# Turning the keys by a transposing transfer and ScalarE in place of TensorE, from the seventh block on

## The chip, the cores and the metric

The kernel runs on one core of one Trainium2 chip. The metric is the time of one execution in device microseconds (us), the median of several runs. Engines are called as in the profile: PE is TensorE (matmuls and transposes), PEld its weight loads, DVE is VectorE, ACT is ScalarE, POOL is GpSimd, and SP is SyncE, which issues the DMA transfers. The engines run side by side; each takes its own instructions in the order fixed when the program is built, and waits on semaphores where it needs another's result.

## What is computed

First a gated linear attention over 4 batches, 8 heads, 768 steps, head size 48, and then a gated MLP with a product along the sequence:

```python
for t in range(S):
    state = alpha[:, :, t, :, None] * state + np.einsum('bhd,bhe->bhde', k[:, :, t], v[:, :, t])
    y[:, :, t] = np.einsum('bhd,bhde->bhe', q[:, :, t], state)
x = y as (batch, 768, 384)
h = gelu_tanh(x @ w_in)                    # 384 -> 1024
u, v = the two halves of h                 # 512 columns each
v_n = (v - mean) / sqrt(var + 1e-06) * g_ln
v_s = np.einsum('ts,bsd->btd', w_sg, v_n) + b_sg
out = x + (u * v_s) @ w_out                # 512 -> 384
```

## The kernel before

**The attention in blocks.** A batch is cut into 6 blocks of 128 steps, 24 blocks in all, numbered i = 0 to 23. The channels of 8 heads lie on 128 partitions, in 3 groups of columns (NK = 3) of 128 steps each; a fourth place per block is filled by two small DMA moves (`last_pair`). For a block the steps are:

- `load_a`, `load_kqv`: the decays and the keys, queries and values come in by DMA.
- `decay` (L405) and `invert` (L427): DVE scans the running product of the decays and its inverse. The inverse lies in a tile with the tag `pi`, of which there are two buffers; that of block i + 2 can be scanned when `scale_k` of block i is done.
- `scale_q` (L418) and `scale_k` (L434): queries times the product, keys times the inverse, in place, 128 x 384 elements each. `scale_k` is the step called ("k", i).
- unit S: 32 small products of keys and queries (L462), masked by DVE (L571).
- unit T: `transposes(i)` turns the scaled keys on PE, three transposes of 128x128 (L566) into PSUM; `k_rows(i)` copies them to the tile `kn` with two ACT copies, of 384 and of 96 elements a partition (L581, L582). This is the step ("kn", i); `kn` has three buffers.
- unit A: products of the masked scores and the values (L477), and the block's gain, values by turned keys (L500, reads `kn`). A waits for the mask and for `kn`.
- units M and H: the rest of the block's output, from the carried state (L477, L488). Between A and M stands `turn` (L544), a tiny ACT instruction that M waits for. DVE then updates the state.

S, A, M and H use 48 or 64 rows of the array and are called tiled here; T and the wide products below use 128.

**The MLP.** Three of the blocks give half a batch's x, split into high and low parts, so that each product is three matmuls (`mm3`, L667 to L669). The wide units are V (x into the second half of h, one per block, followed by GELU, moments, normalisation and a split on ACT, DVE and POOL), U (x into the first half), P (the product along the sequence, 18 matmuls, which needs all six V of the batch) and R (the output product).

**What sets the order.** `ORDER` is a hand-written list of all units of PE. A planner in the kernel (`Plan.issue`) walks through all steps when the program is built: it has a cost in ns for each step, a rule for DMA landings (the issue, plus bytes at 375 a ns, plus 2700 ns for large transfers) and due times from the list; on each engine it takes the step that can start first by its own reckoning, and PE's units at most five places ahead of the list. Several steps have a second engine to go to (`other`), among them the normalisations (ACT or DVE). What comes out is a fixed order of instructions on each engine; at run time only semaphores decide when each starts.

Of the kernel before, what the change touches and what calls it, by code (L numbers as in the profile page):

```python
# [9 lines left out]
F32 = mybir.dt.float32  # L10
F32R = mybir.dt.float32r
BF16 = mybir.dt.bfloat16
I32 = mybir.dt.int32
U32 = mybir.dt.uint32
AF = mybir.ActivationFunctionType
ALU = mybir.AluOpType
PSUM = bass.MemoryType.PSUM

B, H, S, D = 4, 8, 768, 48
DM, DFF = 384, 1024  # L20
HALF = DFF // 2
P = 128
C = 128
C1 = C + 1
NCH = S // C
NP = H // 2
NK = DM // P
# [11 lines left out]
SUMMED = (0, 1)  # L39
EPS = 1e-6  # L40
GEN = 8
LINE, ROOM = 216, 78
NB = 4
SINGLE = 24
R = 64 + D
F64_MIN_AS_F32 = float(np.array(0x38100000, np.uint32).view(np.float32))

ORDER = """
    A0 S0 M0 T2 S2 T0 S1 T1 H0 M1 A1 T3 S3 A2 H2 H1 M2 V01 T4 A3 V00 U002 M3 H3 M4 S4 S5 U000 V02 A4 T5 S6 H4 T7 A5
    T6 A6 S7 V03 H5 M5 M6 V05 U003 A7 H6 V04 M7 P002 P000 S8 H7 U001 U010 P003 U011 U012 T9 P001 U013 P013 T8 P010  # L50
    S9 H8 A9 A8 S10 R000 M8 T10 V10 R002 M9 R001 H9 P011 V12 P012 T11 R011 U101 V13 S11 A10 H10 S12 M10 A11 U103
    R010 M11 A12 V11 H11 M12 H12 T12 S13 U110 U102 T13 V15 P101 V14 U100 U111 R012 P102 A13 P100 S14 P113 P110 R102
    P103 H13 M13 R101 T14 S15 A14 H14 T15 A15 S16 U113 M14 U112 H15 T16 M15 U200 R100 S17 T17 A16 H16 T19 V22 M16
    V24 V20 R112 P111 P112 S18 M17 A17 H17 V21 U201 U202 V23 V25 P200 R110 R111 U203 T18 U210 S19 A19 H18 P203 A18
    S20 M18 T21 H19 P210 T20 M19 R201 P202 P201 R200 U213 A20 S21 T22 U212 A21 H20 S22 M20 H21 U211 P211 U300 M21
    R202 P212 S23 A22 H22 V30 V31 T23 M22 P213 A23 H23 V33 V32 U302 M23 V34 P310 R211 V35 R210 U310 U301 P301 U312
    R212 U311 P313 U313 P312 P302 P300 U303 R302 P303 R311 R300 R301 P311 R310 C0 R312
"""

FIRST = (  # L60
# [131 lines left out]
def tile_gla_gmlp(ctx: ExitStack, tc: tile.TileContext, aT, kqv, w_in, w_sgT, w_out, g_ln, b_sg, out):  # L192
    nc = tc.nc

    const = ctx.enter_context(tc.tile_pool(name="const", bufs=1))
# [6 lines left out]
    att1 = ctx.enter_context(tc.tile_pool(name="att1", bufs=1))  # L202
# [8 lines left out]
    alo2 = const.tile([P, 1], F32, name="alo2")  # L211
    nc.scalar.activation(alo2, warm[:, 0:1], AF.Gelu_apprx_tanh)
    rident = const.tile([P, P], F32R, name="rident")
# [18 lines left out]
    nc.gpsimd.memset(nhalf, -0.5)  # L232
    low = const.tile([P, B * NCH + LINE], F32, name="low")[:, 0:B * NCH]
    pend = const.tile([P, B * NCH, NK], F32, name="pend")
    s_c = const.tile([P, 2, NP, D], F32, name="s_c")
    s_m = const.tile([P, 2, NP, D], F32, name="s_m")

    wi_hi = const.tile([P, 2, NK, HALF], F32R, name="wi_hi")
    wi_lo = const.tile([P, 2, NK, HALF], F32R, name="wi_lo")
# [43 lines left out]
    def split_f64(dst_hi, dst_lo, src, by_pe):  # L283
# [6 lines left out]
        def mag():  # L290
            t["mag"] = stage.tile([P, TH], F32, tag="mag", name="mag", bufs=2)

        def bounded():
            mag()
            nc.scalar.activation(t["mag"], t["raw"][:, :, 1].bitcast(F32), AF.Abs)
            nc.vector.tensor_scalar_max(t["mag"], t["mag"], F64_MIN_AS_F32)
# [20 lines left out]
        def rest():  # L317
            nc.vector.scalar_tensor_tensor(
                dst_lo if by_pe else t["mag"], t["raw"][:, :, 0].bitcast(U32), 2.0 ** -52, t["mag"], op0=ALU.mult, op1=ALU.mult,
            )  # L320
# [58 lines left out]
    st = {}  # L379
    xs = {}  # L380
    groups = [(i,) for i in range(SINGLE)] + [(i, i + 1) for i in range(SINGLE, B * NCH, 2)]

# [38 lines left out]
    def invert_end(i):  # L421
        nc.vector.reciprocal(ends[:, :, C], st[i]["pf"][:, :, C])

    def invert(i):
        s = st[i]
        s["pi"] = pi = att1.tile([P, NK, C1], F32, tag="pi", name="pi", bufs=2)
        nc.vector.tensor_tensor_scan(  # L427
            pi.rearrange("p j t -> p (j t)")[:, ::-1], s["a"][:, NK * C1:0:-1],
            ends.rearrange("p j t -> p (j t)")[:, ::-1], initial=0.0, op0=ALU.mult, op1=ALU.max,
        )  # L430

    def scale_k(i, eng):
        k = st[i]["k"][:, 1:]
        eng.tensor_tensor(k, k, st[i]["pi"][:, :, 1:], op=ALU.mult)  # L434
# [5 lines left out]
    def range_low(i):  # L440
        av = st[i]["a"][:, 0:NK * C1].rearrange("p (j t) -> p j t", t=C1)[:, :, 1:]
        nc.scalar.activation(av, av, AF.Relu, bias=alo, scale=-1.0, accum_out=low[:, i:i + 1])

# [9 lines left out]
    def group(i):  # L453
        return groups[of_group[i]]

    def place(i):
        return group(i).index(i)
# [66 lines left out]
    def carries(i):  # L524
        return i % NCH < NCH - 1
# [33 lines left out]
    def needed(i):  # L559
        return C if carries(i) else 64  # L560
# [16 lines left out]
    def k_rows(i):  # L577
        s = st[i]
        s["kn"] = kn = att1.tile([P, NK * P + 2 * D], F32, tag="kn", name="kn", bufs=3)
        n, tp = needed(i), s["tp"]  # L580
        nc.scalar.copy(kn[0:n, 0:NK * P].rearrange("t (k d) -> t k d", k=NK), tp)  # L581
        nc.scalar.copy(  # L582
            kn[0:n, NK * P:].rearrange("t (e r k) -> t e r k", e=2, k=NK),
            tp.rearrange("t k (e d) -> t e d k", e=2)[:, :, D:],
        )

    def keep_warm(o, n):
        n_col = o.shape[-1]
        moving = warm[:, 0:n_col] if n_col <= P else warm[:, None, :].to_broadcast([P, n_col // P, P])
        for _ in range(n):  # L590
            nc.tensor.matmul(o, warm, moving, start=True, stop=True, skip_group_check=True)

    def state_half(i, on_act=False):
        m = place(i)
        d0, mid = st[group(i)[0]]["dl0"][0:R, m], s_m[0:R, m]
        if i % NCH > 0:
            nc.vector.tensor_tensor(mid, s_c[0:R, m], d0, op=ALU.add)
        elif on_act:
# [4 lines left out]
    def state_add(i):  # L603
        m = place(i)
        nc.vector.tensor_tensor(s_c[0:R, place(i + 1)], s_m[0:R, m], st[group(i)[0]]["dl1"][0:R, m], op=ALU.add)

    def state_decay(i, eng):
        carried = s_c[0:R, place(i + 1)]
        eng.tensor_tensor(carried, carried, st[i]["kq"][0:R, :, 2 * C, None].to_broadcast([R, NP, D]), op=ALU.mult)

# [61 lines left out]
    def mlp_v(x, t, c, summed=False):  # L672
# [7 lines left out]
        def gelu():  # L680
            t["vg"] = mlp.tile([P, HALF], F32, tag="vg", name="vg", bufs=2)
            nc.scalar.activation(t["vg"], t["o"], AF.Gelu_apprx_tanh)

# [17 lines left out]
        def norm_act():  # L701
            nc.scalar.activation(t["vg"], t["vg"], AF.Identity, bias=t["off"], scale=t["rstd"])

# [13 lines left out]
        def gelu_sum():  # L717
            t["vg"] = mlp.tile([P, HALF], F32, tag="vg", name="vg", bufs=2)
            t["sum"] = mlp.tile([P, 2], F32, tag="mv", name="sum", bufs=2)
            nc.scalar.activation(t["vg"], t["o"], AF.Gelu_apprx_tanh, accum_out=t["sum"][:, 0:1])  # L720

# [193 lines left out]
    plan = Plan()  # L915
# [15 lines left out]
    def unit(token):  # L931
# [6 lines left out]
        if kind == "C":  # L938
            return ("R", B - 1, 1, NK - 1, 0), 0
        return (kind, *map(int, rest)), {"U": 1574, "P": 3161, "V": 2091, "R": 2090}[kind]  # L940
# [4 lines left out]
    t = 5000.0  # L945
# [9 lines left out]
    for name, p in pieces:  # L955
        def at(k, name=name):
            return (k,) + name

        if "shift" not in p:
            if name[2] == 1:  # L960
                plan.add(at("load"), "sp", 330, p["load"], takes=[("raw", 2, [at("low")])], nbytes=196608)
            else:
                k = name[1]
# [4 lines left out]
                    takes=[("gl" if k else "gh", 1, [("low", "ws", x, 0) for x in blocks])] if k % ND == 0 else [],  # L968
                    nbytes=196608, due=FIRST.index(("ws", k)) * 20000 - 10**6,
# [14 lines left out]
        last = at("low_pe") if on_pe else at("low")  # L984
# [29 lines left out]
    def first(name):  # L1014
        return FIRST.index(name) * 20000 - 10**6 if name in FIRST else None

    for i in range(n):
# [3 lines left out]
        last = not carries(i)  # L1021
# [3 lines left out]
            nbytes=198656, due=first(("a", i)) or due["S", g[0]] - 15000 + 3000 * m,  # L1025
# [3 lines left out]
            takes=[("kqv", NB, [("H", i)] + ([] if last else [("state", i)]))],  # L1029
            nbytes=394752 if apart else 599552, due=first(("kqv", i)) or due["S", g[0]] - 12000 + 3000 * m,  # L1030
        )
        if apart:
# [5 lines left out]
            takes=[("pf", 2, [("q", i), ("pend", i), ("kept", i), ("end", i)])],  # L1038
# [2 lines left out]
        plan.add(("kept", i), "pool", 100, lambda i=i: decay_kept(i), [("scan", i)])  # L1041
        plan.add(("q", i), "dve*", 550, lambda i=i: scale_q(i), [("scan", i), ("kqv", i)])
        plan.add(("end", i), "dve", 150, lambda i=i: invert_end(i), [("scan", i)] + ([("recip", i - 1)] if i > 0 else []))
        plan.add(("recip", i), "dve*", 960, lambda i=i: invert(i), [("end", i)], takes=[("pi", 2, [("k", i)])])
        by_dve = ("dve*", 550, lambda i=i: scale_k(i, nc.vector))
        by_pool = ("pool", 1150, lambda i=i: scale_k(i, nc.gpsimd))
        plan.add(("k", i), *by_dve, [("recip", i), ("kqv", i)], other=by_pool if b > 0 else None)
# [6 lines left out]
        made = ("A", g[0])  # L1054
        if m == 0:
# [2 lines left out]
            plan.add(  # L1058
                ("turn", i), "act", 190, lambda g=g: turn(g), [made], lead={made: (SLOT if last else 2 * SLOT) - 60 + 410 * len(both[1:])}, keen=300,
            )  # L1060
        plan.add(("kn", i), "act", 740 if not last else 700, lambda i=i: k_rows(i), [("T", i)], takes=[("kn", 3, [made])])
        carried = [("state", i - 1)] if c > 0 else []
        plan.add(
            ("half", i), "dve", 350, lambda i=i: state_half(i), [made] + carried + read_of("m", i), keen=400,
# [2 lines left out]
        if not last:  # L1067
# [13 lines left out]
            takes=[("xf", 3, users)] if head else [],  # L1081
        )
        for e in range(2):
# [3 lines left out]
            takes=[("xh", 2, readers)] if head else [],  # L1087
# [13 lines left out]
    for name, ns in units:  # L1101
        kind, i = name[:2]
# [31 lines left out]
    for b in range(B):  # L1134
# [22 lines left out]
        for hf in range(2):  # L1157
            x = xs[b, hf]
            h = (b, hf)
            for d in range(ND):  # L1160
                u, p = ("U", b, hf, d), ("P", b, hf, d)
# [40 lines left out]
            for kk in range(NK):  # L1202
                r = ("R", b, hf, kk)
# [7 lines left out]
                if (b, hf, kk) == (B - 1, 1, NK - 1):  # L1211
                    for k in range(2):
                        s = st_[4](k)
                        name = r if k == 1 else r + (0,)
# [19 lines left out]
    for k, src in enumerate(words):  # L1234
        t = {}
# [30 lines left out]
    end = due[("P", B - 1, 1, 0)]  # L1266
# [100 lines left out]
```

## Time and profile before

| | |
|---|---|
| time, three runs | median 351.18 us (349.92 to 351.61) |
| span of the profiled execution | 348.3 us; its own time is not listed apart |
| PE busy | 339.9 us, 98% of the span |
| DVE busy | 238.2 us, 68% |
| ACT busy | 156.2 us, 45% |
| POOL busy | 50.0 us, 14% |
| instructions | 10779 |

The span runs from the first to the last instruction of the profiled execution; a run's time has some 2.9 us more around it. A busy time counts an engine's instructions without overlap. In lists of groups a row gives line, engine, operation, tile written <- tiles read, shape, count, then busy us and mean ns of one, and idle time before them with what ended it.

### The profile page before, as it was taken

To read this page: it belongs to the slowest core of one execution; us is meant where nothing else is said; L and a number is where in the kernel's file an instruction comes from. 1 tells how busy PE (TensorE), PEld (TensorE's weight loads), DVE (VectorE), ACT (ScalarE), POOL (GpSimd) and SP (SyncE) were. 2 spreads that over 40 slices of the span, in tenths; PEclk is the share of its full clock that TensorE was granted. 3 is DMA by queue.
4 is the path that set the end of the run, shared out by engine and by line. 5 is a ranking of instruction groups with operands and counts; after the bars stand their busy time and mean duration, and the time that the engine had idled before them with its cause. 6 is when DMAs were issued, how large, how long until landed. Compare 5 with 4: busy or idle time off the path is not lost. (4 is left out here: it accounts for less than half of the span.)

```text
span 348.3 us, 10779 instructions
## 1 busy us (share of the span) xinstructions
PE 339.9 (98%) x4507; PEld 309.5 (89%) x4507; DVE 238.2 (68%) x484; ACT 156.2 (45%) x423; POOL 50.0 (14%) x127
## 2 busy tenths in 40 slices
PE   8898999999999999999999999999999999999996
PEld 4576788899989988999999979999999889999996
DVE  5997988799998668665756788678434667334432
ACT  4564788864433655731225556354132463211100
POOL 2011513410020211300001133101000043000000
PEclk9999999999999999999999999999999999999999
DMA  7948746754336125421234365476200000000012
GB/s 247 388 152 262 219 125 195 223 161 136 104 98 203 36 68 152 118 66 48 71 115 118 103 185 165 135 236 216 68 9 30 8 8 25 23 26 0 2 36 105
DMA packets 23048, 40.80 MB, mean 117 GB/s; under 512 B 3536, under 2 KB 16976, under 8 KB 22992
## 3 DMA queue, kind: packets, MB, share of 16 engines
q1 hardware_dynamic: 22992, 40.05, 37.2%
q8 instruction: 36, 0.59, 0.7%
q14 instruction: 20, 0.16, 0.2%
HBM read 31.77 MB, written 4.72 MB: 105 GB/s over the span
## 5 line engine op out<-in xcount | busy, mean ns | idle before, releaser
L668 PE MATMUL mm_s<-ws_lo,vh 128*128 128x384 f32 x192 | 65.2, 339 | 0.0
L667 PE MATMUL mm_s<-ws_hi,vh 128*128 128x384 f32 x192 | 65.2, 339 | 0.0
L669 PE MATMUL mm_s<-ws_hi,vl 128*128 128x384 f32 x192 | 64.5, 336 | 0.0
L796 DVE SCALAR_TENSOR_TENSOR g<-mm_s,g_col,b_bc 128x384 f32<-128x384 f32 x32 | 19.6, 613 | 26.7 <-PE mm_s L669 26.7
L667 PEld LDWEIGHTS mm_s<-ws_hi,vh 128*128 128x128 f32 x192 | 36.0, 188 | 0.2
L668 PEld LDWEIGHTS mm_s<-ws_lo,vh 128*128 128x128 f32 x192 | 36.1, 188 | 0.0
L669 PEld LDWEIGHTS mm_s<-ws_hi,vl 128*128 128x128 f32 x192 | 36.0, 188 | 0.0
L667 PE MATMUL mm_u<-xh,wi_hi 128*128 128x384 f32 x96 | 33.2, 345 | 0.0
L669 PE MATMUL mm_u<-xh,wi_lo 128*128 128x384 f32 x96 | 32.3, 337 | 0.0
L668 PE MATMUL mm_u<-xl,wi_hi 128*128 128x384 f32 x96 | 32.2, 335 | 0.0
L667 PE MATMUL mm_v<-wi_hi,xh 128*128 128x512 f32 x72 | 29.2, 405 | 0.0
L667 PE MATMUL mm_o<-gh,wo_hi 128*128 128x384 f32 x84 | 28.7, 342 | 0.0
L669 PE MATMUL mm_v<-wi_hi,xl 128*128 128x512 f32 x72 | 28.3, 394 | 0.0
L668 PE MATMUL mm_o<-gl,wo_hi 128*128 128x384 f32 x84 | 28.2, 336 | 0.1
L668 PE MATMUL mm_v<-wi_lo,xh 128*128 128x512 f32 x72 | 28.2, 392 | 0.0
L804 ACT CAST gh<-g 128x384 fp32r<-128x384 f32 x28 | 14.2, 512 | 31.1 <-DVE g L801 24.9
L669 PE MATMUL mm_o<-gh,wo_lo 128*128 128x384 f32 x84 | 28.2, 335 | 0.0
L768 ACT ACTIVATE u<-mm_u 128x384 f32<-128x384 f32 x32 | 15.7, 490 | 27.0 <-PE mm_u L669 27.0
L825 DVE TENSOR_TENSOR r<-mm_o,xf 128x384 f32<-128x384 f32 x23 | 12.5, 551 | 20.8 <-PE mm_o L669 17.2
L405 DVE TENSOR_TENSOR_SCAN pf<-a,floor 128x387 f32<-128x387 f32 x24 | 22.8, 954 | 2.8 <-DMA a<-in_aT 2.7
L477 PEld LDWEIGHTS y<-at,kqv_t 64*64 64x64 f32 x768 | 16.1, 133 | 8.3 <-issue 5.7
L427 DVE TENSOR_TENSOR_SCAN pi<-a,ends 128x387 f32<-128x387 f32 x24 | 23.0, 957 | 0.1
(141 smaller groups left out, 739.9 us busy)
## 6 DMA issues: line engine op xcount, KB each, us to landing
kqv_t<-in_kqv SPq DMA_DIRECT2D x22, 586.0 KB, 4.2
a<-in_aT SPq DMA_DIRECT2D x30, 194.0 KB, 3.0
raw<-in_w_in SPq DMA_DIRECT2D x14, 384.0 KB, 4.6
out_x<-r SPq DMA_DIRECT2D x23, 192.0 KB, 1.9
raw<-in_w_out SPq DMA_DIRECT2D x8, 384.0 KB, 3.3
kqv_t<-kqv_t SPq DMA_DIRECT2D x48, 48.2 KB, 2.2
raw_sg<-in_w_sgT SPq DMA_DIRECT2D x6, 192.0 KB, 5.9
xf<-y SPq DMA_DIRECT2D x48, 24.0 KB, 2.7
```

Source lines behind the costliest of these rows:

```text
L405: nc.vector.tensor_tensor_scan(pf.rearrange("p j t -> p (j t)"), s["a"][:, 0:NK * C1], floor.rearrange("p j t -> p (j t)"), initial=0.0, o ...
L427: nc.vector.tensor_tensor_scan(pi.rearrange("p j t -> p (j t)")[:, ::-1], s["a"][:, NK * C1:0:-1], ends.rearrange("p j t -> p (j t)")[:, : ...
L477: lambda j=j: nc.tensor.matmul(y_of(y, m, j, e)[:, half(h)], v[half(h), D * (2 * j + e):D * (2 * j + e) + 64], at[half(h), e, m, j], start ...
L667: nc.tensor.matmul(o, lh, rh, start=(idx == 0), stop=False)
L668: nc.tensor.matmul(o, lh, rl, start=False, stop=False)
L669: nc.tensor.matmul(o, ll, rh, start=False, stop=(idx == n - 1))
L768: nc.scalar.activation(t["u"], t["o"], AF.Gelu_apprx_tanh)
L796: nc.vector.scalar_tensor_tensor(t["g"], t["o"], g_col[:, d:d + 1], b_bc[:, tsl], op0=ALU.mult, op1=ALU.add,)
L804: nc.scalar.copy(gate_part(g, "h", d), t["g"])
L825: nc.vector.tensor_tensor(t["r"], t["o"], x["xf"][:, kk], op=ALU.add)
```

## The change

Blocks 0 to 5 (`BYPE = 6`) keep T and `k_rows`. For blocks 6 to 23 three steps stand in place of T and `k_rows`: `planes` (ACT) copies the scaled keys, read as 16-bit halves, into two planes of low and high halves, in the block's `pi` tile; `turned` (SP) issues one transposing DMA transfer of 128 x 768 halves from there into a new tile `kt` (two buffers); `k_rows_of` (ACT) joins the halves into `kn` with three copies, of 768 and twice 96 halves. `pi` is now free for the scan of block i + 2 when `turned` of block i has landed. The unit list is a new one, without T6 to T23. The state tiles have one place in place of two (the second was not in use with SINGLE = 24), and two paddings are smaller.

```diff
-LINE, ROOM = 216, 78
+LINE, ROOM = 88, 70
+PLACES = 1 if SINGLE == 24 else 2
+BYPE = 6
...
 ORDER = """
...
+    S9 R001 S10 R000 M9 V12 R002 U102 U100 P011 A10 M10 R011 S11 V13 P012 S12 H10 A11 V14 M11 H11 U103 V15 A12 M12 H12
+    V10 S13 U101 R012 P100 U110 P101 R010 U112 R100 U113 P102 P103 A13 S14 P110 H13 S15 H14 P113 M13 A14 R102 M14 A15
...
-    s_c = const.tile([P, 2, NP, D], F32, name="s_c")
-    s_m = const.tile([P, 2, NP, D], F32, name="s_m")
+    s_c = const.tile([P, PLACES, NP, D], F32, name="s_c")
+    s_m = const.tile([P, PLACES, NP, D], F32, name="s_m")
...
+    def halfwords(t):
+        return t.bitcast(U16)
+
+    def planes(i):
+        s = st[i]
+        s["planes"] = halfwords(s["pi"].rearrange("p j t -> p (j t)"))[:, 0:2 * NK * C]
+        k = halfwords(s["kq"]).rearrange("p j (t two) -> p two j t", two=2)[:, :, 1:, 0:C]
+        nc.scalar.copy(s["planes"].rearrange("p (two j t) -> p two j t", two=2, j=NK), k)
+
+    def turned(i):
+        st[i]["kt"] = kt = att1.tile([P, 2 * NK, P], U16, tag="kt", name="kt", bufs=2)
+        nc.sync.dma_start_transpose(kt, st[i]["planes"])
+
+    def k_rows_of(i):
+        s = st[i]
+        s["kn"] = kn = att1.tile([P, NK * P + 2 * D], F32, tag="kn", name="kn", bufs=3)
+        to, kt = halfwords(kn), s["kt"].rearrange("t (two k) d -> t two k d", two=2)
+        nc.scalar.copy(
+            to[:, 0:2 * NK * P].rearrange("t (k d two) -> t two k d", two=2, k=NK), kt,
+        )
+        for w in range(2):
+            nc.scalar.copy(
+                to[:, 2 * NK * P:].rearrange("t (e r k two) -> t two e r k", e=2, k=NK, two=2)[:, w],
+                kt[:, w].rearrange("t k (e d) -> t e d k", e=2)[:, :, D:],
+            )
...
-        plan.add(("recip", i), "dve*", 960, lambda i=i: invert(i), [("end", i)], takes=[("pi", 2, [("k", i)])])
+        by_pe = i < BYPE
+        plan.add(
+            ("recip", i), "dve*", 960, lambda i=i: invert(i), [("end", i)],
+            takes=[("pi", 2, [("k", i)] + ([] if by_pe else [("turned", i)]))],
+        )
...
-        plan.add(("kn", i), "act", 740 if not last else 700, lambda i=i: k_rows(i), [("T", i)], takes=[("kn", 3, [made])])
+        if by_pe:
+            plan.add(("kn", i), "act", 740 if not last else 700, lambda i=i: k_rows(i), [("T", i)], takes=[("kn", 3, [made])])
+        else:
+            plan.add(("planes", i), "act", 800, lambda i=i: planes(i), [("k", i)])
+            plan.add(
+                ("turned", i), "sp", 600, lambda i=i: turned(i), [("planes", i)], takes=[("kt", 2, [("kn", i)])], nbytes=196608,
+            )
+            plan.add(("kn", i), "act", 1350, lambda i=i: k_rows_of(i), [("turned", i)], takes=[("kn", 3, [made])])
```

## Rows read from the trace of the kernel before

**Rows 1.** The page: span, and each engine's busy us (share) and instructions.
```profile
span 348.3 us, 10779 instructions
PE 339.9 (98%) x4507; PEld 309.5 (89%) x4507; DVE 238.2 (68%) x484; ACT 156.2 (45%) x423; POOL 50.0 (14%) x127
```

**Rows 2.** Stretches: from:to length, busy us of each engine, clock, DMA share, GB/s.
```profile
45.00:71.00 26.00, 25.79 (x522) 21.99 (x521) 21.76 (x46) 22.91 (x66) 7.92 (x19) 1.00 0.57 169
71.00:110.00 39.00, 38.55 (x453) 37.29 (x452) 37.63 (x79) 17.39 (x50) 4.38 (x8) 1.00 0.48 139
110.00:331.00 221.00, 220.78 (x2734) 207.92 (x2734) 136.83 (x274) 89.11 (x235) 28.48 (x70) 1.00 0.28 83
```

**Rows 3.** PE's waits: for whom, us in total, times, longest.
```profile
PE sc L462 <- issue: 1.4, 1, 1.4
...
PE y L488 <- DVE s_m L597: 0.4, 1, 0.4
```

**Rows 4.** PE's timeline, a T between wide products: start, us, instruction.
```profile
172.10 0.34 PE L669 MATMUL mm_o<-gh,wo_lo 128*128 128x384 f32 x1
172.28 0.49 PE L566 MATMUL tp<-ident,kqv_t 128*128 128x128 f32 x3
...
172.79 0.34 PE L668 MATMUL mm_o<-gl,wo_hi 128*128 128x384 f32 x1
...
173.14 0.34 PE L667 MATMUL mm_o<-gh,wo_hi 128*128 128x384 f32 x1
```

**Rows 5.** PE's timeline, from tiled to wide products, with and without T.
```profile
176.47 0.43 PE L488 MATMUL y<-kqv_t,s_m 48*48 48x64 f32 x15
...
177.39 0.33 PE L668 MATMUL mm_u<-xl,wi_hi 128*128 128x384 f32 x1
...
180.54 0.43 PE L488 MATMUL y<-kqv_t,s_m 48*48 48x64 f32 x15
180.90 0.45 PE L667 MATMUL mm_u<-xh,wi_hi 128*128 128x384 f32 x1
181.19 0.34 PE L668 MATMUL mm_u<-xl,wi_hi 128*128 128x384 f32 x1
```

**Rows 6.** The transposes' line: count, durations ns, first and last start.
```profile
L566 PE MATMUL tp<-ident,kqv_t x72: 270/272/332, 7.6 to 273.9; 128*128 128x128 f32 x60, 128*64 128x128 f32 x12
```

**Rows 7.** Groups of ACT copies: busy us, mean ns | idle before, releaser.
```profile
L711 ACT CAST vh<-vg 128x512 fp32r<-128x512 f32 x24 | 14.7, 620 | 11.6 <-DVE vg L706 7.8 <-DVE vg L743 3.7
L634 ACT CAST xh<-xf 128x384 fp32r<-128x384 f32 x24 | 12.2, 515 | 5.5 <-DMA xf<-y 5.2
L581 ACT COPY kn<-tp 128x384 f32<-128x384 f32 (+1 forms) x24 | 11.5, 478 | 6.2 <-PE tp L566 6.1
L582 ACT COPY kn<-tp 128x96 f32<-128x96 f32 (+1 forms) x24 | 5.9, 247 | 0.0
L223 ACT COPY mask<-mask 64x64 bf16<-64x64 bf16 x1 | 0.2, 240 | 0.0
```

**Rows 8.** Timelines of DVE and PE: blocks 6 and 8, keys, scan and A.
```profile
44.72 0.56 DVE L434 TENSOR_TENSOR kqv_t<-kqv_t,pi 128x384 f32<-128x384 f32 x1 [0.26 <-ACT kqv_t L411]
...
54.19 0.96 DVE L427 TENSOR_TENSOR_SCAN pi<-a,ends 128x387 f32<-128x387 f32 x1
...
56.98 0.46 PE L477 MATMUL y<-at,kqv_t 64*64 64x64 f32 x16
...
57.12 0.56 DVE L434 TENSOR_TENSOR kqv_t<-kqv_t,pi 128x384 f32<-128x384 f32 x1
...
95.69 0.46 PE L477 MATMUL y<-at,kqv_t 64*64 64x64 f32 x16
```

**Rows 9.** DMA: the dynamic queue, and issues with size and us to landing.
```profile
q1 hardware_dynamic: 22992, 40.05, 37.2%
a<-in_aT SPq DMA_DIRECT2D x30, 194.0 KB, 3.0
kqv_t<-kqv_t SPq DMA_DIRECT2D x48, 48.2 KB, 2.2
```

More of the change, by code (lines that the diff above doesn't have):

```diff
@@ L14 @@
 U32 = mybir.dt.uint32
+U16 = mybir.dt.uint16
 AF = mybir.ActivationFunctionType
@@ L48 @@
 ORDER = """
[L49 to L57, printed above, removed]
+    M0 S0 S1 A0 T2 T0 S2 H0 M1 H1 A1 T1 M2 S3 T3 A2 V01 H2 A3 V00 T4 U003 T5 S4 M3 M4 H3 S5 U001 A5 A4 M5 V02 H4 S6 H5
+    V03 S7 A6 H6 U000 V05 M7 M6 A7 V04 P000 U010 P001 U011 S8 H7 P003 P002 U002 U013 P013 U012 V11 A8 P010 H8 A9 M8 H9
+    S9 R001 S10 R000 M9 V12 R002 U102 U100 P011 A10 M10 R011 S11 V13 P012 S12 H10 A11 V14 M11 H11 U103 V15 A12 M12 H12
+    V10 S13 U101 R012 P100 U110 P101 R010 U112 R100 U113 P102 P103 A13 S14 P110 H13 S15 H14 P113 M13 A14 R102 M14 A15
+    S16 U111 R101 H15 V22 U200 M15 H16 M16 M17 V20 S17 A16 S18 A17 H17 V21 R111 V23 U201 P112 P111 U202 U203 V25 U210
+    P200 R110 V24 R112 M18 S19 P202 U213 A19 A18 S20 H18 H19 U211 P201 P203 A20 M19 S21 A21 M20 H20 P210 M21 S22 R200
+    U212 H21 U300 U303 R202 R201 P211 P212 V31 S23 P213 V30 A22 V32 H22 M22 R212 A23 U301 V33 H23 M23 R210 P303 V34
+    P300 R211 U310 V35 U312 P310 P312 P301 P302 P313 U302 U313 R301 R300 R310 U311 R311 P311 R312 R302 C0
 """
```

## The prediction

> **What bounds the kernel now.** I read the page's busy shares first: TensorE (PE) is busy 339.9 us of a span of 348.3, ScalarE (ACT) 156.2, VectorE (DVE) 238.2 [rows 1]. A share is an average, so the stretches come next: from 71 to 110 us PE is busy 38.55 of 39, from 110 to 331 us 220.78 of 221, all at granted clock 1.00, its upper level of 2.4 GHz [rows 2]. The list of PE's waits confirms it: the longest step in it, 1.4 us, stands in the first 45 us, and outside the start the longest wait of a product is 0.4 us, once [rows 3]. From 71 us to the branch at the end PE is the bound, and what leaves its queue comes off the span unless something new makes PE wait. What the reader is to see as well: from 45 to 71 us ACT is busy 22.91 of 26 us and PE 25.79 [rows 2]. There the first batch's six V chains, which every spatial product P needs, run on ACT and DVE while PE has little to spare.
>
> The profiled execution's own time is not listed apart from its span. The median of the three runs is 351.18, 2.9 us above the span (1.6 to 3.3 by the runs of 349.92 to 351.61); I work on the span and add 2.9.
>
> **What the change removes.** Three transposes a block for 24 blocks are the 72 of the trace [rows 6]; blocks 6 to 23 lose theirs, 18 units T. A matmul's duration overlaps its neighbours, so I price a T by starts. Where T stands between two wide products, the product before it starts at 172.10 and the second one after it at 172.79: 0.69 us for what takes two slots otherwise, 0.35 (172.79 to 173.14) [rows 4]. That saves 0.34. Where T follows the small 64-row products, it is 176.47 to 177.39, 0.92 us, against 180.54 to 181.19, 0.65, for the same passage without a T [rows 5]: 0.27 saved. In the timeline 12 of the 18 stand the first way and 6 the second: 12 x 0.34 + 6 x 0.27 = **5.7 us** off PE. All lie in the saturated stretches, two of them between 45 and 71 us. ACT's copies out of the transposes' PSUM go too: 478 + 247 ns, some 0.62 us of ACT's time since the second overlaps the first by about 0.1 [rows 7].
>
> **What it adds on ACT.** From 384 to 512 elements an ACT copy grows from 515 to 620 ns [rows 7]: 0.82 ns an element. `planes` moves 768 halves: 515 + 384 x 0.82 = 0.83 us. `k_rows_of` moves 768 and twice 96: 0.83 plus two of about 0.28 (the 247 ns of 96 elements out of PSUM, plus the 37 ns that the SBUF source costs by 515 for L634 against 478 for L581 with the same 384 [rows 7]), less overlap 0.2: 1.2. Together 2.0, against 0.62 before: +1.4 us a block, 18 x 1.4 = 25 us, ACT from 156 to 181 us, 52% of the span. Half of that would remain if 16-bit elements went faster. The one 16-bit copy of the trace, 64 elements in 240 ns [rows 7], lies where the 4-byte line points (515 - 320 x 0.82 = 253), so I take the full price; the row is short and weak evidence. The Trainium skill, "ScalarE: Activation LUTs", section "What ACT_TABLE_LOAD costs", has ScalarE at one element a cycle for 16-bit and 4-byte data alike; by it `planes` is an estimated 186 + 768 x 0.833 = 826 ns, and the sum stays, while a doubled rate for halves would make the addition some 11 us and drop the loss that follows.
>
> What hides it: after 71 us ACT is busy 17.39 of 39 and 89.11 of 221 us [rows 2], so 15 of the 18 blocks find ACT idle more than half the time. Without that cover a block would cost its 1.4 us on PE. Not so from 45 to 71 us. Key scalings end at 45.3 (block 6) and 57.7 (block 8) [rows 8], so blocks 6 to 8 bring 3 x 1.4 = 4.2 us, and planes of block 9 add 0.8: 22.91 + 5.0 = 27.9 in 26 us. Some of ACT's normalisations may go to DVE, busy 21.76 of 26 there [rows 2]; the planner has that choice in its code. Bounds: 0, and the whole overload of about 2 plus queueing of the same size, 4. The first P follows this stretch and waits for the V chains; U products can fill in before it. I take **1.0 us** of loss, nearer to 0, since DVE has 4 us free.
>
> **What it adds on the DMA queues and on the wait for kn.** The trace has no transposing transfer. Below, it is a plain move of 192 KB: the 194 KB load lands 3.0 us after issue. Above, it goes in pieces of 128 halves: 128 rows x 6 = 768 packets. 22,992 packets took 37.2% of 16 engines' 348.3 us, 90 ns each; 768 x 0.09 / 16 = 4.3, plus the 2.2 us in which the small SBUF-to-SBUF pair lands: 6.5 us [rows 9]. I take 4, nearer to the load, because bytes and endpoints are like it. In all 18 x 196,608 B = 3.5 MB come to the 40, and at most 18 x 768 x 0.09 / 16 = 78 us of engine time; after 110 us the engines are busy 0.28 [rows 2], so the loads keep their room.
>
> Latency of the chain k, planes, transfer, kn: 0.8 + 4 + 1.2 and a few tenths of queueing, 6.5 us. Who waits is A, the unit with the gain products. Block 6's key is done at 45.3 and its A starts at 56.98, 11.7 later; that is the shortest distance of the 18. Block 8's are 57.7 and 95.69, 38 us [rows 8]. So A is covered. The planes borrow the buffer of the next-but-one scan of inverses: block 8's scan at 54.19 now waits for block 6's transfer, due near 50.5, so 3.7 us are left [rows 8]; later ones have more. On SP the transfer waits for ACT, and behind it stand loads and pair moves; the due times in the code put a block's loads 12 to 15 us ahead of its S, so a wait of a few us there reaches no unit of PE.
>
> **The order.** Without T, the old unit list changes 77 times between the tiled kinds (S, A, M, H) and the wide ones; the new list 75 times. One round trip fewer costs little: coming out, the first wide slot is 180.90 to 181.19, 0.29 for 0.175 [rows 5], 0.1 more, and I estimate as much for going in: 0.2. The planner moves units within five places, so I take 0 and 1.0 us either way, five trips. The stretch behind the last P holds no T, and both lists end in R products; I change nothing there. Padding, the halved state tiles and U16 views cost nothing: no instruction is added.
>
> Sum: 348.3 - 5.7 + 1.0 = 343.6 of span, + 2.9 = **346.5 us**.
>
> **Rivals.** *Late transfers stop ACT.* The planner fixes ACT's order with kn at 0.6 + 0.5 + 2.7 = 3.8 us after the transfer's issue (its own costs, in the code). ACT takes its instructions in order: when a transfer lands x us later, ACT stands x us, and behind it stand `turn`, for which PE's M waits at once, and the GELUs. One visit to the tiled units comes every 348.3 / 24 = 14.5 us; the chance that its `turn` falls into a stop is x / 14.5 and the mean wait x / 2, so 18 blocks lose 18 x^2 / 29. At x = 2.7, the upper bound above, that is 4.5 us: 351.0, no change. For it: nothing in the trace shows the transfer faster. Against: plain moves land at 2.2 to 3.0 [rows 9]. The same mechanism is the **slower** case: it decides from x = 2.75, a landing 6.6 us after issue, and at x = 4 (7.8 us) loses 9.9: 356.4. The Trainium skill, "Advanced Engine Details and Errata", section "DGE: Hardware vs Software", rates transposes by the hardware descriptor generator below those by the software one, without a figure; that speaks for this rival. Its section "X-Bar Transpose (TRN2)" calls transposing transfers as fast as ordinary ones; by it the landing is an estimated 3.0 us like the load's, and the forecast stands.
>
> *The V chains pay in full.* ACT's overload between 45 and 71 us delays the first P by 4 us: 348.3 - 5.7 + 4 + 2.9 = 349.5. For it: 22.91 of 26 [rows 2]. Against: nothing forces block 8's copies to run there, their A is 38 us away.
>
> *The change frees more.* Fewer round trips, and 1.0 us of crowding avoided: 344.5.
>
> **How the numbers follow.** Forecast 346.5, own range 345 to 348.5: 0.54. Better order, 344 to 345: 0.06. Late transfers with x up to 3.2 (349.4 to 353): 0.14. V chains in full, near 349.5: 0.10. Later still, slower: 0.16. A measurement of this kernel tells about 0.5% from no change, 349.4 to 352.9. Faster: 0.54 + 0.06 + half of the V case 0.05 + 0.04 of the mild late case = 0.69. Same: 0.05 + 0.10 = 0.15. Slower: 0.16. The range 344 to 353 leaves out the slower case and a little below.
>
> **What would show it.** Right: no tp products after block 5, PE busy near 334 us, each step from one wide product to the next without the 0.34; ACT near 181 us; transposing transfers landing within 4.5 us; A never waiting for kn. Wrong: ACT idle before the kn copies with a DMA as the releaser, PE idle behind `turn` (L544's counterpart), or a first P well after 71 us.

## The result, and the profile after

The changed kernel takes 354.51 us (median of 6 runs, 353.01 to 358.2) against 351.14 for the kernel before (6 runs, 349.5 to 351.8): ratio 1.0124, 95% interval 1.0085 to 1.0164. It is slower by about 1%, where the forecast said 346.5 us. The span of the profiled execution went from 348.3 to 353.0 us. A ratio here and below uses the runs within 1.5% of the fastest of the same kernel; that leaves out three of the ten runs of x4, one of x11's ten and one of x10's five.

The page of the changed kernel, its first lines (as [rows 1]):

```profile
span 353.0 us, 10733 instructions
...
PE 337.4 (96%) x4453; PEld 305.1 (86%) x4453; DVE 239.0 (68%) x486; ACT 179.9 (51%) x457; POOL 51.6 (15%) x127
```

The same stretches as [rows 2], of the changed kernel:

```profile
45.00:71.00 26.00, 23.88 (x548) 19.48 (x547) 18.35 (x39) 21.55 (x61) 7.68 (x17) 1.00 0.77 178
71.00:110.00 39.00, 38.40 (x444) 36.48 (x443) 37.23 (x80) 23.29 (x58) 3.86 (x9) 1.00 0.57 143
110.00:331.00 221.00, 215.96 (x2686) 202.62 (x2685) 140.09 (x279) 106.76 (x262) 31.62 (x73) 1.00 0.36 99
```

PE's waits (as [rows 3]), and below them the wait of the kernel before that answers to the first line:

```profile
PE y L479 <- ACT alo L546: 5.3, 7, 1.3
PE y L490 <- DVE s_m L625: 1.9, 2, 1.4
PE sc L464 <- issue: 1.6, 1, 1.6
...
PE mm_v L695 <- ACT xh L662: 0.6, 1, 0.6
```

```profile
PE y L477 <- ACT alo L544: 0.2, 1, 0.2
```

The new ACT groups (as [rows 7]), then the transfers (as [rows 9]) and SyncE's new line, whose times are min/median/max in ns of one issue:

```profile
L606 ACT COPY kn<-kt 128x768 uint16<-128x768 uint16 x18 | 19.3, 1071 | 8.0 <-DMA kt<-pi 7.6 <-PE dl L502 0.3
...
L596 ACT COPY pi<-kqv_t 128x768 uint16<-128x768 uint16 x18 | 15.1, 842 | 3.8 <-DVE kqv_t L436 2.3 <-DVE kqv_t L420 1.3
...
L610 ACT COPY kn<-kt 128x96 uint16<-128x96 uint16 x36 | 8.7, 301 | 0.0
```

```profile
q1 hardware_dynamic: 37392, 43.59, 44.3%
...
kqv_t<-in_kqv SPq DMA_DIRECT2D x22, 586.0 KB, 4.8
...
kt<-pi SPq DMA_TRANSPOSE x18, 2.8
```

```profile
L600 SPq DMA_TRANSPOSE kt<-pi x18: 1209/1262/1756, 46.4 to 251.2; - x18
```

What the reader is to see: the transposes are gone as forecast (4453 products in place of 4507), ACT has the 180 us that the sum gave it, and the transfer lands after 2.8 us (median), sooner than the 4 taken. But PE, which was idle 0.88 us between 45 and 331 us [rows 2], is now idle 2.12 + 0.60 + 5.04 = 7.76 us there. Most of it stands behind `turn` (L546): 5.3 us in 7 waits, 0.2 before. A sign that the prediction named as wrong shows too: ScalarE stands 7.6 us before the kn copies, with the transfer as the releaser (the L606 row), in 6 waits.

A part is the clock. From 32 to 36 us the changed kernel's profiled execution was granted 0.56 and 0.59, the lower level for most of those 4 us, behind a stretch from 30 to 32 us in which PE was busy 1.32 of 2:

```profile
32.00:34.00 2.00, 2.00 (x7) 1.30 (x6) 2.00 (x6) 0.94 (x4) 0.00 (x0) 0.56 0.63 228
34.00:36.00 2.00, 2.00 (x9) 1.73 (x8) 2.00 (x7) 1.10 (x3) 0.00 (x0) 0.59 0.12 22
```

That costs 2 x 0.44 + 2 x 0.41 = 1.7 us. The kernel before had 1.00 there, but a variant of it (b1 below) shows 0.83, 0.50 and 0.81 from 30 to 36 us, so the fall does not need the change. Whether the change makes it more frequent is open: five of the six runs have a mean clock below 0.998, and 30 of the 97 runs of the kernel before in the later sessions, which take 1.2 to 2.6 us longer than the others. As an estimate from these counts, the clock is (5/6 - 30/97) x 1.2 to 2.6 = 0.6 to 1.4 us of the loss; the one of the six runs with a mean clock of 0.999 still took 353.01 us.

### The profile page after: what moved, and what is told of

Read it like the earlier page. It is cut to its first block, busy times and chain, and to the rows that moved or that the text cites. A ratio compares the mean times of both kernels' runs of the same rounds, so it can differ in the third digit from the quotient of the medians.

```text
span 353.0 us, 10733 instructions
## 1 busy us (share of the span) xinstructions
PE 337.4 (96%) x4453; PEld 305.1 (86%) x4453; DVE 239.0 (68%) x486; ACT 179.9 (51%) x457; POOL 51.6 (15%) x127
## 5 line engine op out<-in xcount | busy, mean ns | idle before, releaser
L479 PE MATMUL y<-at,kqv_t 64*64 64x64 f32 x768 | 22.0, 227 | 5.7 <-ACT alo L546 5.3
```

What stands on the lines that cost most here:

```text
L479: lambda j=j: nc.tensor.matmul(y_of(y, m, j, e)[:, half(h)], v[half(h), D * (2 * j + e):D * (2 * j + e) + 64], at[half(h), e, m, j], start ...
```

## One stall followed back

Timelines of PE, ACT, DVE and SyncE's queue, changed kernel, around M16 (start, us, instruction, idle before it and its releaser):

```profile
186.00 1.25 SPq L600 DMA_TRANSPOSE kt<-pi  x1
187.35 0.52 SPq L399 DMA_DIRECT2D kqv_t<-in_kqv  x1
...
191.99 0.56 DVE L420 TENSOR_TENSOR kqv_t<-kqv_t,pf 128x384 f32<-128x384 f32 x1 [1.46 <-DMA kqv_t<-in_kqv]
...
192.59 0.20 ACT L413 COPY kqv_t<-pf 128x3 f32<-128x3 f32 x1 [1.73 <-DVE kqv_t L420]
192.69 0.61 ACT L444 ACTIVATE a<-a,alo 128x384 f32<-128x384 f32 x1
193.21 0.19 ACT L444 ACTIVATION_READ_ACCUMULATOR a<-a,alo 128x1 f32 x1
193.30 0.17 ACT L546 COPY alo<-alo 128x1 f32<-128x1 f32 x1
...
193.53 0.46 PE L479 MATMUL y<-at,kqv_t 64*64 64x64 f32 x16 [1.00 <-ACT alo L546]
```

Read it from the bottom: PE's M waits for `turn`; `turn` stands in ACT's queue behind instructions of another block; these wait for DVE's query scaling; that waits for a load; and the load stood on SyncE behind the issue of a transposing transfer, which held the queue for 1.25 us. The same place in x4_plain, which issues an ordinary transfer of the same bytes:

```profile
185.81 0.53 SPq L600 DMA_DIRECT2D kt<-pi  x1
186.44 0.53 SPq L399 DMA_DIRECT2D kqv_t<-in_kqv  x1
...
190.24 0.53 DVE L420 TENSOR_TENSOR kqv_t<-kqv_t,pf 128x384 f32<-128x384 f32 x1
...
190.81 0.20 ACT L413 COPY kqv_t<-pf 128x3 f32<-128x3 f32 x1 [0.16 <-DVE kqv_t L420]
...
191.52 0.17 ACT L546 COPY alo<-alo 128x1 f32<-128x1 f32 x1
```

The load goes out 0.63 us after its neighbour's start in place of 1.35, it lands 3.5 us after its issue in place of some 4.6 (187.35 to 191.99), DVE finds it there, and PE has no wait from 186 to 195 us. Here two things differ, the later issue (0.7 us) and the longer way of the load (1.1 us). x8_plain_two, which holds SyncE as long with two ordinary transfers, tells them apart:

```profile
185.51 1.24 SPq L603 DMA_DIRECT2D kt<-pi  x2
186.86 0.52 SPq L399 DMA_DIRECT2D kqv_t<-in_kqv  x1
...
190.66 0.56 DVE L420 TENSOR_TENSOR kqv_t<-kqv_t,pf 128x384 f32<-128x384 f32 x1 [0.18 <-DMA kqv_t<-in_kqv]
...
191.97 0.18 ACT L546 COPY alo<-alo 128x1 f32<-128x1 f32 x1
```

The load goes out 1.35 us after its neighbour, as in the changed kernel, but lands in 3.8 us; DVE waits 0.18 us and PE's M not at all. Nor do DVE and M wait here in x11 and x3, which transpose one square of six with a hold of 1.2 us. In x2, with the whole transposing transfer, the load again takes 4.6 us and M waits 0.51. So at this place the hold alone makes no stall; it takes the whole transposing transfer beside the load. That the transfer's packets slow the load is the likely reason; no run shows it by itself.

## The experiments

Three theories stand behind the expectations. A: ACT's added time, or `turn` in ACT's queue, is late in the fixed order. B: the transposing transfers' load on SyncE and on the DMA engines makes loads and small moves late; later split into B1, the held queue, and B2, the packets. C: the new unit list leaves less slack. D, at the end: the planner's costs are to blame, and the mechanism itself gains.

All ratios are against runs of the kernel before on the same chip in the same session (349.7 to 350.1 us there); their 95% intervals are in brackets.

**x1_turn_pool and b1_before_turn_pool: `turn` on POOL**, at its planned place, in the changed kernel and as a control in the kernel before.

```diff
-        st[g[0]]["turn"] = ins = nc.scalar.copy(alo2, alo)
+        st[g[0]]["turn"] = ins = nc.gpsimd.tensor_copy(alo2, alo)
```

> The changed kernel with one edit: the tiny instruction `turn` between A and M is issued on POOL, which is idle 85% of the time, at the place that the plan gave it; all other orders stay. Theory A (in ACT's fixed order `turn` stands behind the new copies and behind ACT's waits for keys and loads, and PE's M waits for it): the 5.3 us that PE waits for `turn` go, 354.5 falls to 349 to 350.5, and PE's waits for L546 are under 1 us. Theory B (the transposing transfers make loads, keys and masks late, whoever waits): the wait moves to H, S or the next product and the time stays at 352.5 or more. Theory C (the new unit list leaves no slack anywhere): as B.

> The kernel before with `turn` issued on POOL, as the control of x1_turn_pool. PE waits only 0.2 us for `turn` there, so nothing is to be won: 350.5 to 351.5 if POOL answers as fast as ACT; if POOL's answer is slower by 0.1 us at each of 24 blocks, 353.5, and x1_turn_pool hides as much.

x1: 355.41 us, ratio 1.0211 [1.0122, 1.0300], four runs, all with a mean clock of 0.986 to 0.995; b1: 350.92, 1.0021 [0.9975, 1.0067]. In x1 PE waits 5.2 us for `turn` on POOL. POOL's queue holds other instructions that wait for ACT and DVE, so moving `turn` moved the wait and did not remove it. But in b1 too PE waits 2.3 us for `turn` on POOL, 0.2 on ACT: POOL brings waits of its own, and x1 does not decide theory A.

**x2_light: ACT's new copies made small.** `planes` copies 16 of 128 steps; `kn` is copied from the keys not turned, as 384 and 96 words, with one element of `kt` read so that it still waits for the transfer.

```diff
-        nc.scalar.copy(s["planes"].rearrange("p (two j t) -> p two j t", two=2, j=NK), k)
+        nc.scalar.copy(s["planes"].rearrange("p (two j t) -> p two j t", two=2, j=NK)[:, :, :, 0:16], k[:, :, :, 0:16])
...
+        nc.scalar.copy(to[:, 1:2], s["kt"][:, NK, 0:1])
+        k = s["k"][:, 1:]
+        nc.scalar.copy(kn[:, 0:NK * P].rearrange("t (k d) -> t k d", k=NK), k)
```

> The changed kernel, same plan and unit list, with ACT's new copies made light: `planes` copies 16 of 128 steps, and `k_rows_of` touches one half-word of the turned keys (so it waits for the same transfer) and then copies the untransposed keys, 384 and 96 words; the gain products so work on wrong keys. About 1 us of ACT a block goes, 18 us in all. Theory A by ACT's busy time: 350 to 351.5, PE's wait for `turn` halved or better. If ACT is late because of what it waits for (keys, loads) and not because of its own time, and for theories B and C: 353.5 to 354.5.

351.06 us, ratio 1.0055 [1.0010, 1.0100]; waits behind `turn` 2.8 us. By time this is what theory A expected. The step from the changed kernel is 0.0069, with an interval of 0.0060 either way, so ACT's copies are a part, and not the whole.

**x3_light_small: x2_light, and one of the six 128x128 squares through the transfer.**

```diff
-        nc.sync.dma_start_transpose(kt, st[i]["planes"])
+        nc.sync.dma_start_transpose(kt[:, NK:NK + 1], st[i]["planes"][:, NK * P:(NK + 1) * P])
```

> As x2_light, and the transposing transfer is cut from 128 x 768 to 128 x 128 halves, the one group that is touched, so SP's issue, the packets and the bytes shrink to about a sixth; the rest of the turned keys is left out. Theory B (SP's 1.26 us an issue against the 0.6 planned, and the load on the DMA engines, make keys late): 2 us or more below x2_light, 348 to 351. Theories A and C: same as x2_light within 1 us.

349.34 us, ratio 1.0003 [0.9962, 1.0044]. It is 1.7 us below x2, less than theory B expected and within the intervals. With neither much copying nor many bytes it only equals the kernel before, although PE has 18 T less (busy 335.0 us). What stayed was SyncE's issue: its median is 1185 ns for the sixth of the transfer.

**x4_plain: an ordinary transfer in place of the transposing one**, everything else as changed. **x5_light_plain: x2_light with that transfer.**

```diff
-        nc.sync.dma_start_transpose(kt, st[i]["planes"])
+        nc.sync.dma_start(kt.rearrange("p k d -> p (k d)"), st[i]["planes"])
```

> Changed kernel with its whole plan, its ScalarE copies and bytes kept, but the 18 transposing transfers issued as ordinary ones of the same 192 KB (kn then holds keys that are not turned). Theory A (only ScalarE's added 1.4 us a block is late in the fixed order): no gain, ratio to the kernel before 1.010 to 1.015, some 354 us. Theory B (the transposing form holds SyncE for 1.26 us an issue where the planner reckons 0.6, and splits into 800 packets, so that loads and the small moves behind it come late): issue back near 0.4 to 0.6 us and packets far fewer, 1.7 to 3 us off: ratio 1.004 to 1.008, 351.5 to 352.8 us. Theory C (the new unit list leaves no slack, whatever the transfer): no gain, as A.

> The run with light ScalarE copies (x2_light, 351.1 us), and now the ordinary 192 KB transfer of x4_plain in place of the transposing one. B: as the run with the sixth of a transfer or a little better, 348.5 to 349.5 us, since the issue time falls too and not only the packets. If the bytes matter and not form or issue: 351 us as x2_light. A and C: no step against x2_light. If A and B together are the whole loss, this one should reach what the removal of T promised, some 345 to 346 us; if it stays near 349 or above, the new unit list (C) or the missing T itself takes the remainder.

x4: 349.57 us, ratio 0.9970 [0.9931, 1.0009]; x5: 346.57 us, ratio 0.9922 [0.9886, 0.9958]. (The profiled executions of x4, span 351.1, and of x5 were the longest of their runs, so sums of waits read from them may be too high.) The form of the transfer alone is worth 1.0124 - 0.9970 = 0.0154, 5.4 us, and with light copies 1.0055 - 0.9922 = 0.0133, 4.7 us, each with an interval of some 0.0057 either way. By the medians, 349.57 and 349.92, x4's ratio is 0.9990, and the form is worth 0.0134. The changed kernel itself was timed in the first session only. SyncE's line and queue in x4, and x5's first lines:

```profile
L600 SPq DMA_DIRECT2D kt<-pi x18: 525/538/1422, 46.7 to 249.4; - x18
...
q1 hardware_dynamic: 25584, 43.59, 39.8%
```

```profile
span 347.4 us, 10721 instructions
...
PE 335.8 (97%) x4453; PEld 304.5 (88%) x4453; DVE 238.6 (69%) x486; ACT 161.3 (46%) x457; POOL 51.7 (15%) x127
```

**x8_plain_two: x4_plain's transfer as two of half the bytes**, so that mainly SyncE's issue time is put back. **x11_small_turn: full ACT copies, one square of six transposed** (the rest of `kn` from keys not turned), so that mainly the packets are taken away.

```diff
+        flat = kt.rearrange("p k d -> p (k d)")
+        for w in range(2):
+            part = slice(w * NK * P, (w + 1) * NK * P)
+            nc.sync.dma_start(flat[:, part], st[i]["planes"][:, part])
```

> x4_plain (349.6 us) with its ordinary 192 KB transfer issued as two of 96 KB, one behind the other: same bytes and form, but SyncE is held twice, about 1.08 us a block where x4_plain has 0.54 and the transposing transfer 1.26. Theory B1 (what hurts is SyncE held by the issue, with loads and small moves queued behind it): three quarters of the 4.9 us come back, some 353 us, ratio 1.007 to 1.012. Theory B2 (what hurts are the transposing transfer's 800 packets on the DMA engines): no change against x4_plain, 349.6 us, ratio 0.994 to 1.000.

> The changed kernel with its full ScalarE copies, but only one of six 128x128 squares goes through the transposing transfer; the copies into kn read the keys not turned (two of three; one small one still reads the transfer's result and so waits for it). SyncE's issue stays at 1.19 us (as x3_light_small showed), the packets fall to a sixth. B1: nearly the time of the changed kernel, 353 to 354.5 us, ratio 1.008 to 1.013. B2: five sixths of the 4.9 us off, some 350.5 us, ratio 0.998 to 1.003. Both parts (x2_light to x3_light_small fell by 1.7 us, x3_light_small to x5_light_plain by 2.8): near 352.5.

x8: 353.68 us, ratio 1.0098 [1.0068, 1.0127]; x11: 352.21 us, ratio 1.0047 [1.0015, 1.0079]. Their issues:

```profile
L603 SPq DMA_DIRECT2D kt<-pi x36: 465/592/677, 46.3 to 251.3; - x36
```

```profile
L600 SPq DMA_TRANSPOSE kt<-pi x18: 1093/1185/1931, 47.3 to 251.2; - x18
```

Two issues of 592 ns hold SyncE 1.18 us a block and bring back 0.0128 of the 0.0154, with ordinary packets (288 a block in place of 144). The second half also goes out 0.6 us later, but ScalarE's waits for the transfer are 7.6 us, 7.2 in x4, so the landing is hardly it. The hold can be read three ways: x4 to x8 0.0128, x4 to x11 0.0077, and x5 to x3 (light copies, an ordinary transfer against one transposed square) 1.0003 - 0.9922 = 0.0081; each is clear of its interval of some 0.005. So the held queue (B1) is shown to cost, 2.7 to 4.5 us, half of the form's price or more. For the rest, the packets (B2), the steps are x11 to the changed kernel 0.0077, x3 to x2 0.0052 and x8 to the changed kernel 0.0026, and only the first is clear of its interval; the stall above points to them at one place. How the two share the price is open. No trace shows place by place where x8 loses against x4.

**x10_act_queue: the transfer issued by ScalarE.**

```diff
-        nc.sync.dma_start_transpose(kt, st[i]["planes"])
+        nc.scalar.dma_start_transpose(kt, st[i]["planes"])
```

> The changed kernel with the transposing transfer issued by ScalarE, right behind planes, in place of SyncE; the plan is kept. B1: SyncE is free of 18 x 1.26 us, 4 to 5 us off, but the issue may hold ScalarE as long, some 20 us more on it, which by the step from the changed kernel to x2_light (3.5 us for some 20 us of copies) gives 4 us back: 350 us if ScalarE's issue is short, 353 to 355 if it is long. B2: packets as before, so nothing is gained, and a long issue makes it worse: 354.5 to 358.

355.9 us (352.56 to 361.74), ratio 1.0157 [1.0123, 1.0192]. The issue holds ScalarE as long as it held SyncE, so this run does not tell B1 from B2. The transfer lands after 4.0 us here. It has a queue to itself, so its time on the DMA engines can be read. First the issue, then the queues (packets, MB, share of 16 engines):

```profile
L600 ACTq DMA_TRANSPOSE kt<-pi x18: 1227/1244/1618, 43.2 to 249.1; - x18
```

```profile
q1 hardware_dynamic: 22992, 40.05, 37.3%
q10 hardware_dynamic: 14400, 3.54, 7.9%
```

One stretch of it is to be seen beside the changed kernel's:

```profile
45.00:71.00 26.00, 25.71 (x517) 21.97 (x510) 21.13 (x43) 24.76 (x67) 9.88 (x21) 1.00 0.76 164
```

With ScalarE's copies as before, but no transfer on SyncE, PE is idle 0.29 us in the crowded stretch, 2.12 in the changed kernel. In part that is a head start: the first transfer is issued at 43.2 us, not 46.4. After 110 us x10 loses as much as the changed kernel (PE busy 215.59 of 221).

**x6_new_list_T: the new unit list with the transposes left on PE** (`BYPE = 24`, T6 to T23 put back at places that I chose so that the planner's steps fit), and **x7_old_list: the change with the old list** less T6 to T23.

```diff
-BYPE = 6
+BYPE = 24
...
-    S8 H7 P003 P002 U002 U013 P013 U012 V11 A8 P010 H8 A9 M8 H9
+    S8 H7 P003 P002 U002 U013 P013 U012 T9 V11 A8 P010 H8 T11 T8 A9 M8 H9
```

> The new unit list with the transposes T6 to T23 put back into it, on TensorE for all 24 blocks: the order alone changes against the kernel before. If the order is worth nothing: 349 to 351.5 us, ratio 0.998 to 1.004. Theory C (the list by itself leaves less slack on ScalarE and VectorE): 353 us or more, ratio above 1.008, with PE waiting behind turn for over 3 us as in the changed kernel (5.3 us there, 0.2 before).

> The old unit list without T6 to T23, and the whole change otherwise: transfers and ScalarE copies for blocks 6 to 23. Theory C: with the old list the waits stay small and the 5.1 us of T come off: 346 to 348 us, ratio below 0.995. Theories A and B: the waits behind ScalarE and SyncE come with the mechanism: 351 us or more, ratio 1.003 to 1.015, PE waiting behind turn and for s_m for 4 us or more in all. The planner has to fit the steps anew to the old list, so this run has another fixed order on each engine than either kernel.

x6: 351.86 us, ratio 1.0061 [1.0029, 1.0094]; x7: 362.87 us, ratio 1.0362 [1.0292, 1.0432]. The new list, with T at my places in it, costs about 0.6%, 2.1 us: theory C in a smaller size than expected. It does so without waits: PE waits 0.5 us behind `turn` and is idle 0.88 us between 45 and 331 us, as in the kernel before; it is busy 340.8 us, 0.9 more. Where the rest of the 2.1 us lies is not shown. x7 tells little about the mechanism: the planner, given a list made for T, makes another order on every engine, and PE's busy time itself rises to 344.5 us, with a mean granted clock of 0.981.

**x9_measured_costs, x12_refit, x13_refit_12: the planner told what the trace shows**, and the list fitted anew. x12 also counts the transfer's time on the DMA engines; x13 has `BYPE = 12` besides.

```diff
-            plan.add(("planes", i), "act", 800, lambda i=i: planes(i), [("k", i)])
+            plan.add(("planes", i), "act", 870, lambda i=i: planes(i), [("k", i)])
...
-                ("turned", i), "sp", 600, lambda i=i: turned(i), [("planes", i)], takes=[("kt", 2, [("kn", i)])], nbytes=196608,
+                ("turned", i), "sp", 1260, lambda i=i: turned(i), [("planes", i)], takes=[("kt", 2, [("kn", i)])], nbytes=281250,
...
-            plan.add(("kn", i), "act", 1350, lambda i=i: k_rows_of(i), [("turned", i)], takes=[("kn", 3, [made])])
+            plan.add(("kn", i), "act", 1420, lambda i=i: k_rows_of(i), [("turned", i)], takes=[("kn", 3, [made])])
```

> The whole change, with three numbers of the planner set to what the trace of the changed kernel shows (planes 870 ns, turned 1260 ns of SyncE where it reckoned 600, kn 1420 ns) and a unit list fitted anew to these. Theory D (the mechanism frees TensorE as forecast, and the loss comes from an order of instructions that was made for a transfer that holds SyncE half as long): the waits behind turn, s_m and xh shrink and the time is 345.5 to 348 us, ratio 0.986 to 0.994. Rival (the added load on SyncE and ScalarE costs what it costs in any order): 350 us or more, ratio 1.000 or more.

> The whole change. The planner's numbers as in x9_measured_costs (planes 870, turned 1260, kn 1420 ns) and the transposing transfer also counted as 281 KB in its one DMA server in place of 197, since x10_act_queue, where this transfer has a queue to itself, shows it on the engines for 7.9% of 350.9 us, 1.54 us a transfer; and the unit list fitted to these with every landing 0.25 us later than reckoned, so that small delays find slack. Theory D' (the loss is an order that does not know how long the transfer holds SyncE and the DMA engines): below the kernel before, 346.5 to 348.5 us, ratio 0.990 to 0.996. Rival (SyncE and ScalarE carry more than any order hides; x9 kept 3.1 us of waits behind turn): 350 to 352 us, ratio 1.000 to 1.006.

> As x12_refit, but blocks 6 to 11 keep their transposes on TensorE (BYPE = 12), so that the crowded stretch of the first batch has neither the transfers nor ScalarE's copies; twelve T are off TensorE in place of eighteen, 1.7 us less gain by the prices of the prediction. If the crowded stretch is where the rest is lost: at or below x12_refit, ratio 0.988 to 0.995. If the cost is the same for every block: between x12_refit and the kernel before.

x9: 351.47 us, ratio 1.0046 [1.0009, 1.0084]; x12: 351.63, 1.0054 [1.0024, 1.0084]; x13: 349.03, 0.9991 [0.9969, 1.0013]. Both expectations of a gain fell. An order that knows the costs gets back some 0.75% (2.6 us), and not the 2.6% between forecast and result. With 12 blocks by transfer the kernel equals the one before, and it is 0.0063 below x12, clear of the intervals: there T on PE for blocks 6 to 11 beat their transfers, though the two have lists of their own. Why x12 is no better than x9 stays partly open. ScalarE no longer stands for the transfer (2.4 us in x9) and PE waits less behind `turn` (3.1 in x9), but PE stands twice where the profile shows no releaser:

```profile
PE y L490 <- issue: 3.6, 2, 1.9
PE y L479 <- ACT alo L546: 1.5, 3, 0.9
```

## Why the prediction was wrong

**T off PE: right.** Taken 5.7 us. With the same unit list PE is busy 340.8 us with T (x6), and 335.9 and 335.0 without it at the same full clock (x2, x3): 4.9 to 5.8 less.

**ACT's sum: right, in part by luck; what it costs: in the bounds, about twice the value taken.** 156 + 25 gave 181, the trace has 179.9; `planes` was priced at 0.83 and takes 0.84, so 16-bit elements go no faster here. But `k_rows_of` was priced at 1.2 and takes 1.42 (183.67 to 185.09), 4 us in 18 blocks, because a copy that writes every second half takes 1.07; against that, 7 normalisations of 0.8 us run on ACT in place of 10. The loss was put at 1.0 us, bounds 0 and 4, for the stretch from 45 to 71 us. Taking the copies away gains 0.0048 (x4 to x5) to 0.0069 (changed kernel to x2), 1.7 to 2.4 us; the first lies within its interval of 0.0053, the second just outside its 0.0060. ACT is busy 21.55 us in that stretch, less than the 22.91 before: it stands behind others (at 62.5 us it had waited 2.56 us for a move of `xf`). The rival *V chains pay in full* would show in the first P, which starts at 73.2 us, 71.3 before. x4 starts it at 73.2 at full clock, x2 at 71.8 and x3 at 70.8: with full copies it comes 1.4 to 2.4 us later, so the rival came in part. The copies alone don't do it: x10 has them and starts its first P at 68.6.

**Latency of the chain and A's cover: right.** The transfer lands in 2.8 us, and PE never waits for the `kn` of blocks 6 to 23. The rival *Late transfers stop ACT*, with a landing more than 6.6 us after issue, did not come as told (2.7 to 5.0). Its sign did: ACT stands 7.6 us for the transfers. It stands 7.2 us for the ordinary ones in x4, so this is not what the form costs. The Trainium skill, "Advanced Engine Details and Errata", section "X-Bar Transpose (TRN2)", has transposing transfers as fast as ordinary ones. The traces don't agree: the landing is 2.8 us against 2.2 for the same bytes in x4, the issue 1.26 us against 0.54, and the time on the engines 1.54 against 0.56 (last section); the measurement decides.

**The step that failed: SyncE and what stands behind the transfer there.** The prediction looked for what is queued behind the transfer while it waits for ACT, and let it go with "a wait of a few us there reaches no unit of PE", since loads are due 12 to 15 us ahead. It never priced the issue itself, and it took the DMA engines to have room for the loads. The issue holds SyncE 1.26 us, 18 times, 0.72 us more than an ordinary one. The wait for ACT is there too: before the 18 issues SyncE stands 21.9 us in all, 10.0 in x4. The cover that the due times promise is not there: in the stall above the load is issued at 187.35, and its reader on DVE is ready 3.2 us later, 1.46 us before it has landed. From DVE the delay passes to ACT, to `turn` and to PE, each in a fixed order. The form of the transfer costs 4.7 to 5.4 us (x2 to x5, changed kernel to x4), half of it or more by the held queue (x8, x11, x3); the rest lies in what else the whole transposing transfer does, its packets beside the loads as far as x11 and the stall show it.

**The order: taken as 0, at most 1.0 either way.** x6 measures 2.1 us of loss (1.0 to 3.3), counting round trips gave 0.2 of gain.

**Sum.** The forecast is a ratio of 346.5 / 351.18 = 0.9867; the result lies 0.0257 above it. Form and copies together are 1.0124 - 0.9922 = 0.0202 in whichever order they are taken, less the 0.003 already taken for the copies; the list adds 0.0061, and T up to 0.002 where it came out smaller: 0.023 to 0.026. The single differences are uncertain by 0.004 to 0.006. So the difference is accounted for within that. The 2.9 us that the prediction adds to the span is 1.7 in the later runs (354.67 against a span of 353.0), so the profiled execution before was the run of 349.92; the forecast difference of 4.7 us does not hang on it.

## What to carry to other kernels

Price an added transfer three times: its landing, the time that its issue holds the queue, and its time on the DMA engines; the landing, which one looks at first, came out better here than it was priced, and the kernel was still slower. In a fixed order an engine that is half idle on average can still pass a delay on, as the stall shows: one engine's wait became the next one's, down to PE. To see which resource an operation costs, put back one at a time: the same bytes in another form, then the same hold with another form. And look at the stall again in that run: here it showed that the hold, which costs time overall, was not enough for this stall.

## What the runs showed of the hardware

- The issue of a transposing SBUF-to-SBUF transfer of 128 x 768 halves holds SyncE 1262 ns, and ScalarE 1244 ns. One square of 128 x 128 takes 1185 ns, so between these two sizes the hold hardly changes. An ordinary transfer of the same 192 KB takes 538 ns.
- It goes in 14400 / 18 = 800 packets and takes 0.079 x 350.9 / 18 = 1.54 us of all 16 DMA engines (x10). The ordinary one takes some (0.398 x 351.1 - 0.372 x 348.3) / 18 = 0.56 us (queue q1 of x4, 39.8%, against [rows 9]), in (25584 - 22992) / 18 = 144 packets.
- A load of a block's keys, queries and values, issued right behind the whole transposing transfer, landed after 4.6 us (x2); the same load landed after 3.5 and 3.8 us behind ordinary ones (x4, x8). This was seen at one place.
- An ACT copy of 768 halves takes 0.84 us when it reads every second half and writes densely, and 1.07 us when it writes every second half, whether it reads densely (changed kernel) or not (1069 ns in x11).
